# Sums of w2, score steps and one softmax put at other places in the planned order of a one-core attention and expert-layer kernel

## The chip, the cores and the metric

The kernel runs on one core of a Trainium2 chip. The metric is the device time of one execution in microseconds; of several runs the median counts. The core has a matrix engine (PE), three elementwise engines (DVE, ACT, POOL) and queues from which transfers are issued (SP above all, POOL and ACT too). Each engine and each queue works through its instructions strictly in the order in which they were written.

## The reference

All numbers are float32. Eight batches of 576 rows go through an attention with 32 memory slots per head, and the result (4608 rows of 512) through four experts with 1024 hidden values each:

```python
a = softmax(phi, axis=2)                          # over the sequence
k_m = einsum('bhsm,bhsd->bhmd', a, k)
v_m = einsum('bhsm,bhsd->bhmd', a, v)
attn = softmax(q @ k_m.T / sqrt(64))
x = (attn @ v_m) as (4608, 512)
p = domain_probs / sum(domain_probs)
for e in range(4):
    out += p[:, e:e+1] * (relu(x @ w1[e]) @ w2[e])
```

## The kernel before

**Products.** Each float32 operand is split into a rounded part and a rest ("high" and "low"), and each product is made of three matmuls (high by high, high by low, low by high). ACT rounds (a cast), DVE or POOL subtracts to get the rest. The product v_m·w1 is made first (`vw`), so that `x @ w1` becomes one product of `vw` with the transposed attention (`AT`).

**Steps.** The work is a list of 512 steps: 4 pairs of batches, 4 experts, 2 batches, 2 halves of a batch (256 and 320 rows), 8 blocks of the hidden layer. `PAIR` is 128 steps. In step s PE makes the hidden block of step s+2 (`first`, L669 to L671; ACT makes the high part with a relu at L681, DVE the low part at L683) and the second product of step s (`second`, L702 to L704). From step 192 on (`BEGIN`) another scheme runs (`unit`, L1041), which makes seven products in place of eight and needs sums and differences of the quarter blocks of w2.

**Work in between.** Everything else is put at step numbers in a table (`plan`), and `run_plan(s)` emits it at the start of step s. Steps 0 to 35 are ordered by a scheduler; from step 36 on the order is the written one. Three tables matter here.

- `JOBS`: (expert, half, step, home, lag). Each job is a call of `sums` (L189): at its step SP loads two blocks of w2 into a tile `raw` (L207, in one of three tiles with the tag `AT`); after `lag` steps DVE makes two sums and two differences in place (L231 to L234, POOL for the last job); in the four steps that follow ACT casts the high parts into a tile `sv` (L219) whose memory is named by `home`, POOL subtracts the rest (L220), and POOL's queue stores both (L225). The home `tl` borrows tiles of the attention.
- `ATT`: for batches 2 to 7 the steps of the attention: the load of phi, `turn` (transposes of the softmaxed phi, then the products with k and v from `turn` + 2 on: a split of the loaded kv by ACT, L351, and POOL, L352, and two steps later the product, L363), the writing of v_m, three score steps (L463; then a copy, a transpose, the maximum, the exponential, the sum and the scaling in the six steps behind it), and three transposes of the result (L541).
- `stage_ahead` (L134): kv, q and the weights to be split are loaded by SP into four stage tiles, in the order in which the plan takes them, three ahead of the one taken. A load waits until the tile used four loads before it is free again.

**Start.** The first batch's attention is written out by hand (from L1163 on). There `scores_exp`, `vw_out` of the first head pair and `soft` follow each other.

Of the kernel before, what the change touches and what calls it, by code (L numbers as in the profile page):

```python
# [10 lines left out]
F32R = mybir.dt.float32r  # L11
# [7 lines left out]
N, DM, E, F = 4608, 512, 4, 1024  # L19
P = 128  # L20
# [8 lines left out]
PAIR = E * STEPS  # L29
LAST = NG * PAIR  # L30
STAGE = 4
KVS = 3
# [18 lines left out]
PAIR_AT = ((18, 19, 26, 27), (28, 29, 30, 31))  # L51

ATT = {
    2: (22, 30, 48, (101, 107, 112), (114, 115, 119)),
    3: (38, 46, 65, (116, 118, 120), (PAIR + 2, PAIR + 4, PAIR + 6)),
    4: (88, 96, 114, (PAIR + 71, PAIR + 75, PAIR + 79), (PAIR + 81, PAIR + 85, PAIR + 93)),
    5: (107, PAIR - 2, PAIR + 16, (PAIR + 83, PAIR + 87, PAIR + 91), (PAIR + 118, PAIR + 124, PAIR + 128)),
    6: (PAIR + 3, PAIR + 14, PAIR + 32, (2 * PAIR + 99, 2 * PAIR + 103, 2 * PAIR + 107), (2 * PAIR + 109, 2 * PAIR + 113, 2 * PAIR + 117)),
    7: (PAIR + 18, PAIR + 32, PAIR + 50, (2 * PAIR + 111, 2 * PAIR + 115, 2 * PAIR + 119), (2 * PAIR + 125, 2 * PAIR + 127, 2 * PAIR + 128)),
}  # L60

UNITS_1 = (1, 5, 5, 6, 5, 6, 8, 9, 10, 11, 11, 12, 17, 13, 13, 20)
# [8 lines left out]
Q = 256  # L71
X_BANK, Y_BANK, AB_BANK = 4, 2, 6
JOBS = (
    (2, 0, 34, "w1", 5), (2, 1, 60, "tl", 4), (3, 0, 85, "w1", 5), (3, 1, 104, "kvs", 5),
    (0, 0, PAIR + 2, "w1", 5), (0, 1, PAIR + 33, "w1", 5), (1, 0, PAIR + 48, "kvs", 4),
    (1, 1, PAIR + 62, "kvs", 4),
)
KEEP_AT, W2_AGAIN = (20, 12, -1, 20), 24
FOUR_AT_7 = ((0, 4, 8, 12), (16, 20, 24, 28))
# [6 lines left out]
def body(ctx: ExitStack, tc: tile.TileContext, qm, qt, kv, kvt, phi, prob, w1, w1d, w2, out):  # L86
    nc = tc.nc
    pool = lambda name, **k: ctx.enter_context(tc.tile_pool(name=name, bufs=1, **k))
    const, wp, work, att = pool("const"), pool("wp"), pool("work"), pool("att")
# [103 lines left out]
    def sums(e, fh, s, home, lag):  # L193

        kept = []
        top, low = slice(0, Q), slice(Q, DM)
        late = s + lag > BEGIN
        v = nc.gpsimd if late else nc.vector
        sub = v.tensor_sub

        def load():
            tag = {"tag": "a"} if home == "tl" else {"tag": "AT", "bufs": 3}
            t = att.tile([P, 2, 2, DM], F32R, name="raw", **tag)
            kept.extend(t[:, i].bitcast(F32) for i in range(2))
            kept.append(t)
            for i in range(2):
                nc.sync.dma_start(kept[i], w2[e, 2 * fh + i])  # L207

        def high(i, j):
            if j == 0:  # L210
                if home == "tl":
                    width, tag = ((DM, "tl"), (640, "ph"))[i]
                    t = att.tile([P, 2, width], F32R, name="sv", tag=tag)
                    t = t.rearrange("p a c -> p (a c)")[:, :2 * DM].rearrange("p (a c) -> p a c", a=2)
                else:
                    pool, bufs = (wp, 4) if home == "w1" else (att, KVS)
                    t = pool.tile([P, 2, DM], F32R, name="sv", tag=home, bufs=bufs)
                kept.append(t)
            nc.scalar.copy(kept[3 + i][:, j], kept[i][:, j])  # L219
            nc.gpsimd.tensor_sub(kept[2][:, i, j], kept[i][:, j], kept[3 + i][:, j].bitcast(F32))  # L220

        def store(i):
            d = dram.tile([P, 2, 2, DM], F32, name=f"v{e}{fh}{i}")
            for r, src in enumerate((kept[3 + i], kept[2][:, i])):
                nc.gpsimd.dma_start(d[:, :, r], src.bitcast(F32))  # L225
            for j in range(2):
                kept_for["v", e, fh, 2 * i + j] = d[:, j]

        at(s, load)
        s += lag  # L230
        at(s, lambda: v.tensor_add(kept[1][:, :, low], kept[0][:, :, low], kept[1][:, :, low]))  # L231
        at(s + late, lambda: sub(kept[0][:, :, low], kept[0][:, :, top], kept[0][:, :, low]))
        at(s + 1 + late, lambda: sub(kept[0][:, :, top], kept[1][:, :, low], kept[0][:, :, top]))
        at(s + 1 + 2 * late, lambda: sub(kept[1][:, :, top], kept[1][:, :, top], kept[0][:, :, top]))  # L234
        s += 3 * late
        for i in range(2):
            for j in range(2):
                at(s + 1 + 2 * i + j, lambda i=i, j=j: high(i, j))
            at(s + 3 + 2 * i, lambda i=i: store(i))
# [211 lines left out]
    def tiles(t0):  # L451
        return (2, P) if t0 < 4 else (1, 64)
# [45 lines left out]
    def scores_exp(b, t0):  # L498
        nt, n = tiles(t0)
        av = st["at", b, t0][:n, :nt * H, :]  # L500
        nc.scalar.activation(av, av, AF.Exp, scale=float(D) ** -0.5)

    def soft_sum(b, t0):
        nt, n = tiles(t0)
        av = st["at", b, t0][:n, :nt * H, :]
        zv = st["mx", b, t0][:n, :nt * H]
        nc.vector.reduce_sum(guarded[:n, :nt * H, 0], av, AX.X)
        nc.vector.reduce_sum(zv[:, :, 0], guarded[:n, :nt * H], AX.X)
        nc.vector.reciprocal(zv[:, :, 0], zv[:, :, 0])
# [6 lines left out]
    def soft(b, t0):  # L516
        soft_sum(b, t0)
        soft_scale(b, t0, nc.vector)
# [59 lines left out]
    def vw_out(ps, k, e, fh, hp, odds, last=True):  # L578
        to = [(vw_tile(k, e, odd, fh, hp // 2), vw_rows(2 * k + odd, hp)) for odd in odds]
        for t, r in to:  # L580
            nc.scalar.copy(t[r, 0, :], ps[r])
        for t, r in to:
            nc.vector.tensor_sub(t[r, 1, :], ps[r], t[r, 0, :].bitcast(F32))  # L583
        if last:
            give(ps)
# [146 lines left out]
    def at(s, unit):  # L732
        plan[s].append(unit if isinstance(unit, tuple) else (None, unit))
# [427 lines left out]
    with tc.manual_schedule():  # L1161
        raw = {key: take(later) for later, key in enumerate(early)}
        stage_ahead(len(early) + 4)  # L1163
        nc.scalar.copy(att.tile([P, 1], F32, name="woken", tag="woken"), ident[:, :1])
        nc.sync.dma_start(pt, prob)
        keep_warm(10)
        dve, gps = nc.vector, nc.gpsimd
        for g in range(2):
            phi_max(0, g)
        for g in range(2):  # L1170
            phi_exp(0, g)
        kvr = lambda hp: raw["kv", 0, hp]
        for g in range(2):
            phi_norm(0, g)
        kv_split(0, 0, kvr(0), 0, gps)
        kv_split(0, 0, kvr(0), 1, dve)
        phi_turn(0, 0)
        phi_turn_out(0, 0)
        tail_split(0, raw["kvt", 0], 0, gps)
        phi_turn(0, 1)  # L1180
        phi_turn_out(0, 1)
        kv_split(0, 1, kvr(1), 0, dve)
        kv_split(0, 1, kvr(1), 1, gps)
        phi_turn_tail(0)
        phi_turn_tail_out(0)
        tail_split(0, raw["kvt", 0], 1, gps)
        for c2 in range(2):
            kv_split(0, 2, kvr(2), c2, dve)
        kv_split(0, 3, kvr(3), 0, dve)
        for hp in range(2):  # L1190
            for c2 in range(2):
                kv_mm(0, hp, c2)
            kv_mm_tail(0, hp)
        kv_split(0, 3, kvr(3), 1, dve)
        for hp in range(2):
            kv_out(0, hp)
        for hp in (2, 3):
            for c2 in range(2):
                kv_mm(0, hp, c2)
            kv_mm_tail(0, hp)  # L1200
            if hp == 2:
                for i in range(2):
                    kv_fold(0, i)
        keep_warm(3)
        kv_pick(0, 0)
        w1g = [raw["w1", 0, 0, g] for g in range(2)]
        split_w1(w1g[0], 0, 0, gps)
        for hp in (2, 3):
            kv_out(0, hp)
        write_vt_0(0, slice(0, 1))  # L1210
        q = raw["qm", 0, 0]
        scores_mm(0, 0, q, (0, 1))
        for hp in (2, 3):
            kv_fold(0, hp)
        keep_warm(5)
        kv_pick(0, 1)
        scores_mm(0, 0, q, (2, 3))
        scores_copy(0, 0)
        scores_turn(0, 0)
        scores_max(0, 0)  # L1220
        split_w1(w1g[0], 0, 1, gps)
        write_vt_0(0, slice(1, 2))
        keep_warm(2)
        split_w1(w1g[1], 0, 2, gps)
        split_w1(w1g[1], 0, 3, gps)
        pv = [vw_mm(0, 0, hp, ("p2", 4)) for hp in range(4)]
        scores_exp(0, 0)
        vw_out(pv[0], 0, 0, 0, 0, (0,))
        soft(0, 0)
        keep_warm(3)  # L1230
        for hp in (1, 2):
            vw_out(pv[hp], 0, 0, 0, hp, (0,))
        transposes(0, 0)
        keep_warm(4)
        transposes_out(0, 0)
        vw_out(pv[3], 0, 0, 0, 3, (0,))
        for i in range(2):
            split_w2(0, 0, i, raw["w2", 0, 0], gps)
        for s in range(AHEAD):
            first(s)  # L1240
        probabilities()
# [78 lines left out]
```

## Time and profile before

| What | Value |
|---|---|
| Median of 3 runs | 1383.67 us (1383.65 to 1386.94) |
| The profiled execution's own time | 1382.22 us |
| Its span, first to last instruction | 1380.4 us |
| PE's mean granted clock | 0.993 |
| Instructions | 26287 |
| Read from and written to memory | 221.85 MB, 84.93 MB |

The page gives each engine's busy time. The windows view gives the same by stretches, with the granted clock (PEclk) as a share of full speed. The timeline lists instructions in order of time: start, duration, engine, line, operation, tiles, and in square brackets how long the engine was idle before it and what ended that. Step 60 falls at about 230 us, step 98 at 329 us and step 110 at 367 us.

### The profile page before, as it was taken

How to read it: one execution, taken by the hardware profiler on the slowest of the kernel's cores; microseconds unless marked ns; L12 is line 12 of the kernel's file. 1: busy time of each engine (PE TensorE's matmuls, PEld its weight loads, DVE VectorE, ACT ScalarE, POOL GpSimd, SP SyncE). 2: the span in 40 equal slices, each digit the busy share in tenths (PEclk: the TensorE clock that was granted, in tenths of full speed). 3: DMA queues.
4: the chain of work that ended last, by engine and by line, in shares of the span. 5: the costliest groups of instructions: out<-in, count | busy, mean ns of one | idle time of the engine just before them, and what ended most of it. 6: DMA issues, size and time to landing. Idle time of an engine off the chain costs nothing.

```text
span 1380.4 us, 26287 instructions
## 1 busy us (share of the span) xinstructions
PE 1348.2 (98%) x9294; PEld 1237.0 (90%) x9294; DVE 852.1 (62%) x1920; ACT 658.0 (48%) x1594; POOL 693.8 (50%) x743
## 2 busy tenths in 40 slices
PE   7999999899899999999999999999999999999998
PEld 6778888787778888889999999999999999999998
DVE  7875635343545445457767766666667766666666
ACT  7765565445445655444445455555543333333332
POOL 4400474757443634446467677767754434334432
PEclk9999999999999999999999999999999999999999
DMA  6752375897578354464589999999983866666552
GB/s 258 250 187 76 116 247 180 310 311 240 164 255 295 123 179 155 168 248 150 176 275 317 373 331 320 320 311 325 340 282 130 255 178 180 180 182 177 168 172 75
DMA packets 104340, 309.84 MB, mean 224 GB/s; under 512 B 25232, under 2 KB 26384, under 8 KB 104208
## 3 DMA queue, kind: packets, MB, share of 16 engines
q1 hardware_dynamic: 83472, 232.65, 53.6%
q0 software_dynamic: 19584, 71.31, 13.2%
q10 hardware_dynamic: 1152, 4.19, 0.8%
q8 instruction: 74, 1.21, 0.4%
q14 instruction: 58, 0.48, 0.1%
HBM read 221.85 MB, written 84.93 MB: 222 GB/s over the span
## 4 chain that ended last, share of the span: by engine, by line
PE 86%; DVE 5%; issue 3%; POOL 2%; ACT 2%; DMA 1%; POOLq 0%; ACTq 0%; DVEq 0%
PE banks L1041 28%; PE banks L702 6%; PE banks L704 6%; PE banks L703 6%; PE banks L955 6%; PE banks L956 6%; PE banks L957 6%; PE banks L669 3%; PE banks L670 3%; PE banks L671 3%; PE banks L607 2%; PE banks L363 2%; DVE vw L583 1%; PE banks L1080 1%; PE banks L1079 1%
## 5 line engine op out<-in xcount | busy, mean ns | idle before, releaser
L1059 DVE SCALAR_TENSOR_TENSOR acc<-banks,pt,acc 128x256 f32<-128x256 f32 x528 | 253.0, 479 | 137.0 <-PE banks L1041 132.5
L164 POOL TENSOR_TENSOR w<-stage,w 128x512 fp32r<-128x512 f32 x134 | 175.4, 1315 | 141.2 <-ACT w L163 133.0
L1041 PE MATMUL banks<-w,a 128*128 128x256 f32 x1344 | 192.4, 282 | 0.0
L955 PE MATMUL banks<-AT,vw 128*128 128x256 f32 (+1 forms) x640 | 189.3, 296 | 0.0
L956 PE MATMUL banks<-AT,vw 128*128 128x256 f32 (+1 forms) x640 | 188.9, 295 | 0.0
L957 PE MATMUL banks<-AT,vw 128*128 128x256 f32 (+1 forms) x640 | 188.9, 295 | 0.0
L1041 PEld LDWEIGHTS banks<-w,a 128*128 128x128 f32 x1344 | 178.8, 189 | 4.9
L683 DVE SCALAR_TENSOR_TENSOR h<-banks,h 128x256 fp32r<-128x256 f32 x192 | 80.6, 420 | 132.3 <-ACT h L681 84.7
L1022 POOL TENSOR_TENSOR vt<-ph,vt 128x512 fp32r<-128x512 f32 x80 | 103.4, 1292 | 114.9 <-ACT vt L1021 84.6
L702 PE MATMUL banks<-w,h 128*128 128x512 f32 x384 | 152.8, 398 | 1.7 <-ACT h L681 1.7
L703 PE MATMUL banks<-w,h 128*128 128x512 f32 x384 | 152.1, 396 | 0.7 <-POOL w L164 0.7
L704 PE MATMUL banks<-w,h 128*128 128x512 f32 x384 | 151.5, 395 | 0.8 <-DVE h L683 0.8
L681 ACT ACTIVATE h<-banks 128x256 fp32r<-128x256 f32 x192 | 73.4, 383 | 124.1 <-PE banks L671 104.5
L1007 ACT ACTIVATE a<-banks 128x512 fp32r<-128x512 f32 x80 | 47.9, 598 | 173.4 <-DVE ph L1013 130.5
L1032 POOL TENSOR_TENSOR tl<-xs,tl 128x256 fp32r<-128x256 f32 x80 | 59.1, 739 | 133.3 <-ACT tl L1031 72.4
L669 PE MATMUL banks<-AT,vw 128*128 128x320 f32 (+1 forms) x384 | 118.8, 310 | 5.3 <-DVE h L683 3.0
L956 PEld LDWEIGHTS banks<-AT,vw 128*128 128x128 f32 x640 | 120.7, 189 | 0.1
L955 PEld LDWEIGHTS banks<-AT,vw 128*128 128x128 f32 x640 | 120.5, 188 | 0.2
L957 PEld LDWEIGHTS banks<-AT,vw 128*128 128x128 f32 x640 | 120.3, 188 | 0.0
L352 POOL TENSOR_TENSOR kvs<-stage,kvs 128x512 fp32r<-128x512 f32 x58 | 75.3, 1317 | 87.1 <-ACT kvs L351 80.0
L670 PE MATMUL banks<-AT,vw 128*128 128x320 f32 (+1 forms) x384 | 114.4, 298 | 0.0
L671 PE MATMUL banks<-AT,vw 128*128 128x320 f32 (+1 forms) x384 | 113.9, 298 | 0.0
(154 smaller groups left out, 3128.0 us busy)
## 6 DMA issues: line engine op xcount, KB each, us to landing
w<-kw SPq DMA_DIRECT2D x92, 512.0 KB, 5.2
vwd<-vst POOLq DMA_DIRECT2D x80, 512.0 KB, 6.4
vw<-vwd SPq DMA_DIRECT2D x320, 128.0 KB, 5.8
w<-v SPq DMA_DIRECT2D x68, 512.0 KB, 5.9
stage<-in_w SPq DMA_DIRECT2D x44, 512.0 KB, 4.5
stage<-in_w1d SPq DMA_DIRECT2D x40, 512.0 KB, 5.2
stage<-in_kv SPq DMA_DIRECT2D x32, 512.0 KB, 4.4
kw<-w POOLq DMA_DIRECT2D x24, 512.0 KB, 5.1
```

The costliest lines, as they stand in the source:

```text
L164: eng.tensor_sub(dst[:, 1, :], raw, dst[:, 0, :].bitcast(F32))
L669: nc.tensor.matmul(ps, w[:, 0, f], at_t[:, g, 0, c], start=g == 0, stop=False)
L670: nc.tensor.matmul(ps, w[:, 0, f], at_t[:, g, 1, c], start=False, stop=False)
L671: nc.tensor.matmul(ps, w[:, 1, f], at_t[:, g, 0, c], start=False, stop=g == 1)
L702: nc.tensor.matmul(po[t], x[:, 0, :], w[:, 0, :], start=j == 0, stop=False)
L703: nc.tensor.matmul(po[t], x[:, 0, :], w[:, 1, :], start=False, stop=False)
L704: nc.tensor.matmul(po[t], x[:, 1, :], w[:, 0, :], start=False, stop=j == NJ - 1)
L955: nc.tensor.matmul(ps, w[:, 0, f], at_t[:, g, 0, c], start=g == 0, stop=False)
L956: nc.tensor.matmul(ps, w[:, 0, f], at_t[:, g, 1, c], start=False, stop=False)
L957: nc.tensor.matmul(ps, w[:, 1, f], at_t[:, g, 0, c], start=False, stop=g == 1)
L1041: nc.tensor.matmul(ps, a[:, l, jj], w[:, r, c], start=start and jj + i == 0, stop=jj == 1 and i == 2, skip_group_check=True,)
L1059: VE.scalar_tensor_tensor(a, src, p, a, ALU.mult, ALU.add)
```

## The change

No matmul, cast or subtraction is added or removed; the softmax sums are the same. What changes is where the work stands.

```diff
-    2: (22, 30, 48, (101, 107, 112), (114, 115, 119)),
+    2: (22, 30, 48, (93, 97, 102), (111, 112, 113)),
...
-    (2, 0, 34, "w1", 5), (2, 1, 60, "tl", 4), (3, 0, 85, "w1", 5), (3, 1, 104, "kvs", 5),
+    (2, 0, 18, "kvs", 3), (2, 1, 34, "w1", 5), (3, 0, 85, "w1", 5), (3, 1, 98, "w1", 5),
...
-            tag = {"tag": "a"} if home == "tl" else {"tag": "AT", "bufs": 3}
-            t = att.tile([P, 2, 2, DM], F32R, name="raw", **tag)
+            t = att.tile([P, 2, 2, DM], F32R, name="raw", tag="AT", bufs=3)
...
         scores_exp(0, 0)
+        soft(0, 0)
         vw_out(pv[0], 0, 0, 0, 0, (0,))
-        soft(0, 0)
```

- **Jobs.** Expert 2's first job goes from step 34 to 18 (home kvs, lag 3), its second from step 60 (home tl) to the freed step 34; expert 3's second from 104 to 98 (home w1). The branch for the home tl is deleted. Three later jobs stand three steps earlier: steps 158, 173 and 187, the last with a lag of 6 instead of 4.
- **Batch 2.** Scores at steps 93, 97, 102 instead of 101, 107, 112; transposes at 111, 112, 113 instead of 114, 115, 119.
- **Batch 4.** `turn` goes from step 96 to 99, with all that hangs on it.
- **Batches 4 to 7, after step 192.** Score steps mostly five apart instead of four, with the transposes shifted by one to eight steps.
- **Start.** The softmax of the first scores stands ahead of the first `vw_out`.

On POOL, at steps 94 to 104. The tiles `w` are weights being split, `kvs` and `tl` the kv of batch 4, `at` the scores of batch 2, `raw` the sums of w2. Before:

```order
L164 TENSOR_TENSOR w_3407<-stage,w_3407 128x512
L164 TENSOR_TENSOR w_3432<-stage,w_3432 128x512
L338 TENSOR_TENSOR tl<-stage,tl 64x512 x2
L164 TENSOR_TENSOR w_3463<-stage,w_3463 128x512
L352 TENSOR_TENSOR kvs<-stage,kvs 128x512 x2
L164 TENSOR_TENSOR w_3495<-stage,w_3495 128x512
L164 TENSOR_TENSOR w_3515<-stage,w_3515 128x512
L352 TENSOR_TENSOR kvs<-stage,kvs 128x512 x4
```

and now:

```order
L164 TENSOR_TENSOR w_3425<-stage,w_3425 128x512
L164 TENSOR_TENSOR w_3449<-stage,w_3449 128x512
L164 TENSOR_TENSOR w_3482<-stage,w_3482 128x512
L164 TENSOR_TENSOR w_3508<-stage,w_3508 128x512
L508 TENSOR_TENSOR at<-at,mx 128x512
L164 TENSOR_TENSOR w_3536<-stage,w_3536 128x512
L332 TENSOR_TENSOR tl<-stage,tl 64x512 x2
L346 TENSOR_TENSOR kvs<-stage,kvs 128x512 x2
L508 TENSOR_TENSOR at<-at,mx 128x512
L346 TENSOR_TENSOR kvs<-stage,kvs 128x512 x2
L214 TENSOR_TENSOR raw<-raw,sv 128x512 x2
```

The first kv splits now stand behind all weight splits of this stretch, and the subtractions of expert 3's second job stand among the kv splits.

On SP, at steps 92 to 100. `vw` are tiles read back from memory, `in_qm` is q, `in_kvt` and `in_kv` the kv of batch 4, `raw` the blocks of w2. Before:

```order
L646 DMA vw<-vwd_3242 32x1024
L149 DMA stage<-in_kv 128x1024
L149 DMA stage<-in_w 128x1024
L149 DMA stage<-in_qm 128x1024
L149 DMA stage<-in_kv 128x1024 x2
```

and now:

```order
L640 DMA vw<-vwd_3242 32x1024
L149 DMA stage<-in_qm 128x1024
L149 DMA stage<-in_w 128x1024
L149 DMA stage<-in_kvt 128x1024
L149 DMA stage<-in_kv 128x1024
L206 DMA raw<-in_w 128x1024 x2
L149 DMA stage<-in_qt 128x256
```

The load that stood first behind the `vw` loads was kv; in its place, and so in its stage tile, now stands the q of batch 2's second score step.

On ACT, at steps 110 and 111. `h` and `hm` are the relus that the second product waits for, `sv` the casts of a w2 job, `at` the exponential of the scores, `ph,zs` that of phi. Before:

```order
L163 CAST w_3826<-stage 128x512
L376 COPY xs<-banks 64x128 x2
L219 CAST sv<-raw 128x512
L681 ACTIVATE hm<-banks 128x64
L681 ACTIVATE h<-banks 128x256
L163 CAST w_3864<-stage 128x512
L501 ACTIVATE at<-at 128x512
L281 ACTIVATE ph,zs<-ph,nm 128x576 x2
L219 CAST sv<-raw 128x512
```

and now:

```order
L163 CAST w_3856<-stage 128x512
L370 COPY xs<-banks 64x128 x2
L345 CAST kvs<-stage 128x512 x2
L385 COPY kvm_78<-banks 128x128
L675 ACTIVATE hm<-banks 128x64
L675 ACTIVATE h<-banks 128x256
L163 CAST w_3895<-stage 128x512
L275 ACTIVATE ph,zs<-ph,nm 128x576 x2
```

The two casts `sv` and the exponential `at` are gone from here; a kv split and a copy have come.

More of the change, by code (lines that the diff above doesn't have):

```diff
@@ L53 @@
 ATT = {
-    2: (22, 30, 48, (101, 107, 112), (114, 115, 119)),
+    2: (22, 30, 48, (93, 97, 102), (111, 112, 113)),
     3: (38, 46, 65, (116, 118, 120), (PAIR + 2, PAIR + 4, PAIR + 6)),
[L56 to L59, printed above, removed]
+    4: (88, 99, 117, (PAIR + 71, PAIR + 76, PAIR + 81), (PAIR + 79, PAIR + 84, PAIR + 94)),
+    5: (107, PAIR - 2, PAIR + 16, (PAIR + 86, PAIR + 91, PAIR + 96), (PAIR + 118, PAIR + 124, PAIR + 128)),
+    6: (PAIR + 3, PAIR + 14, PAIR + 32, (2 * PAIR + 99, 2 * PAIR + 103, 2 * PAIR + 108), (2 * PAIR + 110, 2 * PAIR + 114, 2 * PAIR + 118)),
+    7: (PAIR + 18, PAIR + 32, PAIR + 50, (2 * PAIR + 112, 2 * PAIR + 116, 2 * PAIR + 123), (2 * PAIR + 120, 2 * PAIR + 125, 2 * PAIR + 131)),
 }
@@ L73 @@
 JOBS = (
-    (2, 0, 34, "w1", 5), (2, 1, 60, "tl", 4), (3, 0, 85, "w1", 5), (3, 1, 104, "kvs", 5),
-    (0, 0, PAIR + 2, "w1", 5), (0, 1, PAIR + 33, "w1", 5), (1, 0, PAIR + 48, "kvs", 4),
-    (1, 1, PAIR + 62, "kvs", 4),
+    (2, 0, 18, "kvs", 3), (2, 1, 34, "w1", 5), (3, 0, 85, "w1", 5), (3, 1, 98, "w1", 5),
+    (0, 0, PAIR + 2, "w1", 5), (0, 1, PAIR + 30, "w1", 5), (1, 0, PAIR + 45, "kvs", 4),
+    (1, 1, PAIR + 59, "kvs", 6),
 )
@@ L210, in high @@
             if j == 0:
[L211 to L217, printed above, removed]
+                pool, bufs = (wp, 4) if home == "w1" else (att, KVS)
+                t = pool.tile([P, 2, DM], F32R, name="sv", tag=home, bufs=bufs)
                 kept.append(t)
```

## The prediction, made before the changed kernel had run

> **What bounds the kernel now.** I read the page's busy times first, then its chain, then the windows, then the timeline of each engine wherever the windows show PE idle.
>
> ```profile
> PE 1348.2 (98%) x9294; PEld 1237.0 (90%) x9294; DVE 852.1 (62%) x1920; ACT 658.0 (48%) x1594; POOL 693.8 (50%) x743
> ...
> PE 86%; DVE 5%; issue 3%; POOL 2%; ACT 2%; DMA 1%; POOLq 0%; ACTq 0%; DVEq 0%
> ...
> 0.00:60.00 60.00, 49.42 (x307) 40.18 (x308) 47.06 (x95) 44.11 (x103) 25.09 (x28) 0.94 0.70 251
> 240.00:260.00 20.00, 15.98 (x87) 13.46 (x86) 7.83 (x17) 8.74 (x22) 18.83 (x21) 1.00 0.85 302
> 320.00:340.00 20.00, 16.59 (x96) 14.23 (x94) 6.18 (x15) 11.87 (x29) 19.65 (x18) 0.95 0.67 227
> 340.00:360.00 20.00, 20.00 (x138) 16.60 (x137) 7.21 (x20) 8.78 (x26) 7.10 (x6) 0.96 0.78 247
> 360.00:380.00 20.00, 16.49 (x98) 14.13 (x97) 10.91 (x28) 8.80 (x25) 9.26 (x9) 0.89 0.32 93
> 380.00:400.00 20.00, 18.86 (x105) 15.16 (x104) 8.77 (x24) 11.24 (x32) 10.04 (x11) 0.94 0.61 215
> 620.00:700.00 80.00, 78.50 (x672) 73.61 (x671) 58.63 (x140) 34.23 (x82) 44.28 (x49) 1.00 0.53 172
> 1060.00:1080.00 20.00, 18.99 (x163) 16.98 (x163) 15.15 (x37) 7.24 (x20) 8.85 (x10) 1.00 0.57 173
> ```
>
> A window's row gives its length, then the busy time of PE, weight loads, DVE, ACT and POOL, then PE's granted clock. PE is busy for 1348.2 of 1380.4 us and the change alters none of its work, so all it can win is the 32.2 us of idle PE and the stretches at a lowered clock. Those lie in few places: 10.6 us at the start, 4.0 at 240 to 260, 3.4 at 320 to 340, 3.5 and 1.1 at 360 to 400, 1.5 and 1.0 later. The clock is down at the start and from 320 to 400 only.
>
> **A: the w2 sum at step 60.** It moves away.
>
> ```profile
> 252.63 0.50 PE L703 MATMUL banks<-w,h 128*128 128x512 f32 x1 [0.67 <-POOL w L164]
> 257.65 0.50 PE L607 MATMUL banks<-w,vs 128*128 128x512 f32 x1 [3.36 <-POOL w L164]
> ...
> 249.88 0.62 ACT L163 CAST w<-stage 128x512 fp32r<-128x512 f32 x1
> ...
> 248.59 0.72 POOL L225 DMA_DIRECT2D v<-sv  x1
> 249.76 1.59 POOL L220 TENSOR_TENSOR raw<-raw,sv 128x512 fp32r<-128x512 f32 x1
> 254.64 0.93 POOL L225 DMA_DIRECT2D v<-sv  x1
> 255.82 1.78 POOL L164 TENSOR_TENSOR w<-stage,w 128x512 fp32r<-128x512 f32 x1
> ```
>
> PE waits twice, 0.67 and 3.36 us, for weight splits that POOL makes late. Ahead of them POOL does four subtractions of the job (1.3 to 1.6 us each) and four store issues (about 0.6 us each, the distance of the rows at 254.64 and 255.82 being two of them): 8 us in all. Without them the split of 255.82 is ready 8 us sooner, and what is late next is ACT's cast, done at 250.5, before PE asks at 253.9. **A is worth 4.0 us.**
>
> The job goes to step 34, where one of the same shape stood; that one goes to step 18.
>
> ```profile
> 136.10 1.28 POOL L338 TENSOR_TENSOR tl<-stage,tl 64x512 fp32r<-64x512 f32 x1 [57.68 <-ACT tl L337]
> ...
> 100.00:120.00 20.00, 20.00 (x106) 17.11 (x105) 8.13 (x22) 4.49 (x15) 0.00 (x0) 1.00 0.17 61
> ...
> 104.96 0.33 SPq L149 DMA_DIRECT2D stage<-in_w  x1
> 122.97 0.33 SPq L149 DMA_DIRECT2D stage<-in_w  x1
> ```
>
> POOL has nothing to do for 57.7 us there, and DVE and ACT are idle for 11.9 and 15.5 of the 20 us from 100 on, so four operations on each are hidden. If none were, DVE's four at 0.69 us would cost 2.8; I take 0. On SP the load for step 34 now stands between the two weight loads shown. It must wait until the first job's stores have freed its tile; from 104.96 to 122.97 SP has 18 us for that.
>
> **B: batch 4's kv product.**
>
> ```profile
> 336.13 0.74 PE L363 MATMUL banks<-kvs,a 128*128 128x256 f32 x4 [2.89 <-POOL kvs L352]
> 339.14 0.63 PE L702 MATMUL banks<-w,h 128*128 128x512 f32 x1
> ...
> 330.98 2.52 POOL L338 TENSOR_TENSOR tl<-stage,tl 64x512 fp32r<-64x512 f32 x2
> 333.59 1.26 POOL L164 TENSOR_TENSOR w<-stage,w 128x512 fp32r<-128x512 f32 x1
> 334.81 2.52 POOL L352 TENSOR_TENSOR kvs<-stage,kvs 128x512 fp32r<-128x512 f32 x2
> ...
> 333.75 0.62 ACT L163 CAST w<-stage 128x512 fp32r<-128x512 f32 x1 [3.70 <-DMA stage<-in_w]
> ```
>
> PE stands for 3.4 us (by the window) because POOL is behind, and then runs at half clock (a 512 matmul takes 0.63 us, 0.40 elsewhere). The windows from 320 to 360 lose 0.05 and 0.04 of 20 us, 1.8 us. **B costs 5.2 us.** The product now comes three steps of about 2.2 us later, with two score steps (about 0.9 us of PE each) ahead of it and 0.8 us of phi transposes already there before: near 341 us on the old scale instead of 333. POOL, from 330.9 on, has four weight splits (5.2), one scaling (1.05), two tl (2.5) and two kvs (2.5) to do: done at 342 at the latest, and the product's first half needs only the first of the two kvs. I count B as gone, with nothing to spare; bounds 0 to 5.2.
>
> **The q of step 97 is new there.** SP's load behind the `vw` loads waits for the stage tile of a weight block that POOL splits at steps 93 and 94.
>
> ```profile
> 324.51 0.35 SPq L149 DMA_DIRECT2D stage<-in_kv  x1
> 326.01 0.60 PE L307 MATMUL banks<-ident,ph 128*128 128x128 f32 x4
> ...
> stage<-in_qm SPq DMA_DIRECT2D x16, 512.0 KB, 4.7
> ```
>
> Before, this was kv and had time. Now it is q, issued at 324.5 and landed 4.7 us later (median of the q loads) at 329.2. PE, whose step 97 began with the row at 326.01, asks at 326.6 (a score step and its transpose, 0.9, less one phi transpose, 0.35, come ahead). **I expect a new wait of 2.5 us**, 0 if POOL gets there sooner, 4.6 with the slowest load of that stretch (6.8 us). It gives POOL the time that B lacked.
>
> Whether the clock falls with it is open: 3.36 us of idle left it at 1.00 in 240 to 260, 2.89 lowered it at 336. The Trainium skill, page "TensorE: Matmul & The Clock Gate", section "Part 1: The HAM clock gate", says that the clock halves after an idle window of about 3.4 us, and that the windows run free of the program. The trace agrees that length alone does not decide. By that rule a wait of 2.5 us leaves the clock alone and the sum below stands; by the row at 336 it would be 1.8 us more.
>
> **C: steps 110 to 112.**
>
> ```profile
> 376.55 0.64 PE L669 MATMUL banks<-AT,vw 128*128 128x320 f32 x1 [3.01 <-DVE h L683]
> ...
> 370.55 0.68 DVE L233 TENSOR_TENSOR raw<-raw 128x512 f32<-128x512 f32 x1
> ...
> 371.31 0.62 ACT L219 CAST sv<-raw 128x512 fp32r<-128x512 f32 x1 [3.36 <-issue]
> 373.38 0.77 ACT L281 ACTIVATE ph<-ph,nm 128x576 f32<-128x576 f32 x1
> 375.52 0.38 ACT L681 ACTIVATE h<-banks 128x256 fp32r<-128x256 f32 x1
> ```
>
> ACT stands 3.4 us before a cast of expert 3's second job, whose input DVE makes only at 371.2, behind scores and phi maxima. The relus wait behind that cast, and then behind two exponentials of phi, one of scores and another cast; PE idles 3.5 us in this window. The clock loses 0.11 and 0.06 of 20 us, 3.4, of which up to 1.5 falls into idle time: 1.9 to 3.4, I take 2.6. **C costs 6.1 us.** The job's casts go to steps 104 to 107 and the scores earlier, so phi's exponentials stand alone. What comes in at 110 (a kv split of 1.2 us and a copy) fits a step. At 104 the same wait exists in small: ACT's first cast stands behind DVE's accumulation. I take C as gone and 1.0 us as the price of the fuller steps 101 to 113 (bounds 0 and 5.2, a stall like B).
>
> **Small terms.** At 380 to 400 PE idles 1.1 us beside batch 2's transposes and scores, which leave: 1.0 won. At the start:
>
> ```profile
> 29.67 0.66 PE L541 MATMUL banks<-ident,at 128*128 128x128 f32 x4 [2.49 <-DVE at L514]
> ...
> 26.23 0.68 DVE L583 TENSOR_TENSOR vw<-banks,vw 64x512 fp32r<-64x512 f32 x1
> 27.63 0.68 DVE L164 TENSOR_TENSOR w<-stage,w 128x512 fp32r<-128x512 f32 x1
> 28.39 0.63 DVE L164 TENSOR_TENSOR w<-stage,w 128x512 fp32r<-128x512 f32 x1
> ```
>
> Three pieces of other work, some 1.9 us, leave the softmax's way, but the eviction put behind it then stands ahead of the next thing PE needs: 0.8 won, bounds 0 and 2.5. The later score steps stand beside 1.5 and 1.0 us of idle; four of their waits cannot all go: 0.6 won, bounds -1 and 2.5.
>
> **Sum.** 4.0 + 5.2 + 6.1 + 1.0 + 0.8 + 0.6 = 17.7 won, 2.5 + 1.0 = 3.5 lost, 14.2 net. The profiled execution took 1382.2 us (span 1380.4 and 1.8 around it), so 1368.0; the median of the runs is 1.5 above it: **1369.5 us**.
>
> **Rivals.**
> - *One stall comes back*, as kv splits, sums and weights crowd POOL at 101 to 108, or with the q wait at half clock: 5.2 us, 1374.7. For it speaks that B's sum leaves nothing to spare.
> - *Everything goes well*: q in time, the start and the late steps at their upper bounds, 2.5 + 1.7 + 1.9 more: 1363.4. Against it speaks the row at 324.51.
> - *The amount, not the order, makes B and C*: POOL is busy for 19.65 of 20 us at 320 to 340, and what it must do by step 113 is the same. Then the stalls only move, and A and the small terms less the q wait remain, 3 us: 1380.5, within what can be told from no change. Against it: POOL is busy for only 7.1 of the next 20.
> - *Slower*: SP stands at the load for step 34 until the stores of step 18's job land, with two weight loads and all of batch 2's kv behind it. From 123 us on each us late may reach PE; it eats the gain at 137 and makes the kernel slower by over 0.3% (4.2 us, about what can be told from no change) at 141.5. With a landing 20 us late: 1375 to 1390. Against it: some 18 us of room.
>
> **How the numbers follow.** Forecast (1365 to 1372.5) 0.56; one stall back (1372.5 to 1379) 0.21; all well (1360 to 1365) 0.09; only moved (1379.5 to 1387.8) 0.09; slower 0.05. The first three are faster by over 0.3%: 0.86. The range leaves out a tenth at each end: 1362 to 1379.
>
> **What would show it.** The windows 240 to 260 and 350 to 390 with PE at 20.0 and the clock at 1.00 show A, B and C gone. A wait of step 97's score product on the load of q, of 1 to 4 us near 320 us, shows the new one. A wait of the kv product or of the hidden block on POOL or DVE near 335 to 350 us shows the first rival; SP idle past 123 us at the load of `raw` the last. The forecast is wrong if PE idles over 3 us at a place not named here.

## The result, and the profile after

| What | Before | After |
|---|---|---|
| Median of 4 runs | 1384.0 us (1383.65 to 1386.94) | 1369.43 us (1368.16 to 1369.53) |
| Ratio, 95% interval | | 0.9888 [0.9871, 0.9905] |
| Span of the profiled execution | 1380.4 us | 1367.6 us |

The forecast was 1369.5 us. That it is met this closely is luck: the start cost 7.5 us more than forecast, smaller terms came out better by 6.3 us together, and the place of the two profiled executions among the runs made up the rest (the sum is below). One execution of this study, the profiled one of the kernel e11_turn96, took 2179.74 us at a granted clock of 0.556; its ratio leaves that execution out, and no drift of it is given.

The page's busy times and windows of the changed kernel (length, busy PE, weight loads, DVE, ACT, POOL, then PE's granted clock, DMA share and GB/s):

```profile
PE 1346.5 (98%) x9294; PEld 1236.9 (90%) x9294; DVE 852.1 (62%) x1920; ACT 658.1 (48%) x1594; POOL 695.1 (51%) x743
...
60.00:80.00 20.00, 16.49 (x90) 13.86 (x89) 9.66 (x28) 10.23 (x31) 5.03 (x4) 0.83 0.69 244
240.00:260.00 20.00, 20.00 (x113) 17.56 (x112) 8.49 (x19) 10.09 (x25) 15.23 (x18) 1.00 0.80 282
320.00:340.00 20.00, 19.88 (x133) 16.88 (x134) 10.04 (x24) 14.64 (x34) 19.55 (x18) 1.00 0.89 299
340.00:360.00 20.00, 19.99 (x129) 17.55 (x128) 12.12 (x30) 10.50 (x33) 15.15 (x14) 1.00 0.87 285
360.00:380.00 20.00, 19.85 (x114) 17.34 (x114) 8.90 (x28) 12.42 (x36) 10.59 (x10) 1.00 0.47 166
380.00:400.00 20.00, 19.44 (x145) 15.54 (x144) 8.74 (x18) 7.26 (x21) 6.59 (x10) 1.00 0.60 213
```

From 240 to 400 the stalls are gone and the clock stays at 1.00. The window 60 to 80 lost 3.5 us of PE and has its clock at 0.83; before, it stood at 20.00 and 1.00. That stall was in no term of the forecast.

**The drift.** Where the time went is read more sharply from one instruction that both kernels run 192 times in the same order: DVE's low part of the relu of hidden block k. For block 18 the timelines of DVE say, before and after:

```profile
96.24 0.41 DVE L683 SCALAR_TENSOR_TENSOR h<-banks,h 128x256 fp32r<-128x256 f32 x1
```

```profile
102.89 0.41 DVE L677 SCALAR_TENSOR_TENSOR h<-banks,h 128x256 fp32r<-128x256 f32 x1
```

so the changed kernel is 6.65 us late there. The same difference at five more blocks (the expectations below call block k "step k"), in us against the kernel before:

```
block            9     18     72     81     90    123
changed       -0.1    6.7    6.9    2.0    2.0  -10.9
```

Between blocks 9 and 18 it loses 6.8, between 72 and 81 it wins 4.9 (A), between 90 and 123 it wins 12.9 (B, C and the small term), and behind block 123 another 1.9, to 12.8 in all, the difference of the spans. Between blocks 90 and 123 moved work cancels only at the end, so the figures within that stretch are not read one by one.

**The lost stretch.** Timelines of SP, ACT and PE in the changed kernel, from 59 to 70 us:

```profile
59.51 0.33 SPq L149 DMA_DIRECT2D stage<-in_w  x1
...
61.45 0.22 ACT L675 ACTIVATE hm<-banks 128x64 fp32r<-128x64 f32 x1
66.05 1.14 ACT L163 CAST w<-stage 128x512 fp32r<-128x512 f32 x2 [4.38 <-DMA stage<-in_w]
67.09 0.61 ACT L345 CAST kvs<-stage 128x512 fp32r<-128x512 f32 x1
67.61 0.53 ACT L370 COPY xs<-banks 64x128 f32<-64x128 f32 x2
...
68.19 0.48 PE L378 MATMUL banks<-ident,xs 128*128 128x128 f32 x1 [3.26 <-ACT xs L370]
69.58 0.63 PE L698 MATMUL banks<-w,h 128*128 128x512 f32 x1
```

PE waits 3.26 us for copies on ACT. ACT could have made them at 63.6, when PE had finished their banks, but it stands at two casts of a weight whose load was issued at 59.51, 6.5 us before they could begin. Then PE runs at about half its speed (a 512 matmul takes 0.63 us, 0.40 elsewhere; the clock of this window is 0.83). These are steps that the scheduler orders, and in the kernel before it had put the copies ahead of the second of these casts, and the load ahead of one of two phi loads.

### The profile page after: what moved, and what is told of

Same layout as the page of the kernel before. It is cut to its first block, busy times and chain, and to the rows that moved or that the text cites. A ratio compares the mean times of both kernels' runs of the same rounds, so it can differ in the third digit from the quotient of the medians.

```text
span 1367.6 us, 26263 instructions
## 1 busy us (share of the span) xinstructions
PE 1346.5 (98%) x9294; PEld 1236.9 (90%) x9294; DVE 852.1 (62%) x1920; ACT 658.1 (48%) x1594; POOL 695.1 (51%) x743
## 3 DMA queue, kind: packets, MB, share of 16 engines
q8 instruction: 74, 1.21, 0.4%
## 4 chain that ended last, share of the span: by engine, by line
PE 90%; DVE 4%; ACT 3%; DMA 2%; issue 2%; POOL 0%; SPq 0%; ACTq 0%; DVEq 0%; POOLq 0%
PE banks L1035 29%; PE banks L698 6%; PE banks L696 6%; PE banks L697 6%; PE banks L949 6%; PE banks L950 6%; PE banks L951 6%; PE banks L663 3%; PE banks L665 3%; PE banks L664 3%; PE banks L601 3%; PE banks L357 2%; PE banks L1074 1%; PE banks L1073 1%; PE banks L1075 1%
## 5 line engine op out<-in xcount | busy, mean ns | idle before, releaser
L663 PE MATMUL banks<-AT,vw 128*128 128x320 f32 (+1 forms) x384 | 118.3, 309 | 3.6 <-DVE vw L577 1.7
L1035 PE MATMUL banks<-w,vt 128*128 128x256 f32 x768 | 113.9, 281 | 0.2 <-DVE acc L1053 0.2
L664 PE MATMUL banks<-AT,vw 128*128 128x320 f32 (+1 forms) x384 | 113.3, 296 | 0.0
```

The costliest lines, as they stand in the source:

```text
L663: nc.tensor.matmul(ps, w[:, 0, f], at_t[:, g, 0, c], start=g == 0, stop=False)
L664: nc.tensor.matmul(ps, w[:, 0, f], at_t[:, g, 1, c], start=False, stop=False)
L1035: nc.tensor.matmul(ps, a[:, l, jj], w[:, r, c], start=start and jj + i == 0, stop=jj == 1 and i == 2, skip_group_check=True,)
```

## The experiments

The kernels of the experiments were each timed in five rounds against the kernel before. "Gain" is one minus the ratio, times 1384 us, with its 95% interval; A is the drift from block 72 to 81, "middle" that from 90 to 123, "start" that from 9 to 18 (negative is a gain), in one profiled execution each.

| Kernel | Median us | Gain us | start | A | middle |
|---|---|---|---|---|---|
| changed kernel | 1369.43 | 15.5 (13.1 to 17.9) | 6.8 | -4.9 | -12.9 |
| e1_noswap | 1364.36 | 18.0 (15.2 to 20.8) | 0.0 | -4.9 | -12.9 |
| e2_swap | 1389.5 | -5.3 (-7.1 to -3.5) | 7.1 | 1.2 | 0.2 |
| e3_sum | 1367.07 | 16.5 (14.7 to 18.3) | 1.6 | -4.9 | -13.0 |
| e12_problate | 1365.99 | 16.7 (13.4 to 20.1) | 0.5 | -4.9 | -13.0 |
| e4_jobs2 | 1377.99 | 5.8 (4.2 to 7.3) | 0.0 | -4.9 | 0.6 |
| e5_mid | 1372.78 | 11.5 (8.7 to 14.3) | 0.0 | 2.4 | -13.0 |
| e6_b2j3 | 1372.58 | 11.8 (9.6 to 14.1) | 0.0 | -0.3 | -11.5 |
| e7_phi4b2 | 1374.83 | 9.1 (7.1 to 11.1) | 0.0 | 1.3 | -9.1 |
| e9_b2 | 1374.31 | 10.4 (7.9 to 12.7) | 0.0 | 1.2 | -9.4 |
| e10_j3 | 1380.24 | 4.0 (2.6 to 5.5) | 0.0 | 2.3 | -4.8 |
| e8_late | 1382.76 | 1.4 (0.1 to 2.8) | 0.0 | 1.2 | -0.8 |
| e11_turn96 | 1366.57 | 18.7 (15.5 to 21.9) | | | |

Kernels that leave a stretch as it was show how far one execution scatters: A lies between -0.3 and 2.4 in them, "middle" between -0.8 and 0.6.

### The stall at 68 us

**e1_noswap**, the changed kernel without the swap:

```diff
-        soft(0, 0)
         vw_out(pv[0], 0, 0, 0, 0, (0,))
+        soft(0, 0)
```

> The changed kernel without the swap at the start (the eviction ahead of the softmax's sum again); all tables as in the change. Theory: the 3.26 us stall at 68 us and the half clock behind it, 6.7 us between the relus of steps 9 and 18, come from the swap, because the ordered steps 0 to 35 then come out in another order (two phi loads ahead of a weight load on SP, both casts of that weight ahead of four copies on ACT). Then this kernel loses the stall and keeps everything else: 1369.4 - 6.7 = 1362.7 us, 0 to 0.8 more for the start, and the window 60 to 80 has PE at 20.0 at clock 1.00. Rival: the stall comes from expert 2's first job, now at step 18, whose loads and stores crowd the same stretch: then it stays and the time is 1369 to 1371.

The stall is gone and the start drifts by 0.0; the median is 1364.36, against 1362.7 to 1363.5 expected.

**e2_swap**, the kernel before with the swap alone:

```diff
+        soft(0, 0)
         vw_out(pv[0], 0, 0, 0, 0, (0,))
-        soft(0, 0)
```

> The kernel before with the swap at the start alone. Theory (the swap makes the stall): 1384.0 + 6.7 = 1390.7 us, and PE waits 3 us for the copies of the kv product near 68 us. Rival (the job at step 18 makes it): within 1 us of before, 1383 to 1384, by the 0.8 us that the prediction gave the swap.

Slower by 5.3 us (3.5 to 7.1), with the same wait, in its timeline of PE:

```profile
70.31 0.47 PE L384 MATMUL banks<-ident,xs 128*128 128x128 f32 x1 [3.58 <-ACT xs L376]
```

The theory holds, the time a little below its 1390.7: the swap alone makes the stall, and no job is needed for it.

**e3_sum** keeps half of the swap and **e12_problate** all of it, and both come out of the scheduler in other orders:

```diff
-        soft(0, 0)
+        soft_sum(0, 0)
         vw_out(pv[0], 0, 0, 0, 0, (0,))
+        soft_scale(0, 0, nc.vector)
```

> The changed kernel with only the sum and the reciprocal of the softmax ahead of the eviction and its scaling behind it. On ACT the second pair of kv copies then stands ahead of the casts of the late weight again; on SP the two phi loads still stand ahead of that weight's load. Theory that ACT's order makes the stall: it is gone, 1362 to 1363.5. Rival that the later load alone makes it: the stall stays, smaller, and the time is 1366 to 1369.

```diff
-        probabilities()
     load_phi(1)
+    probabilities()
```

> The whole changed kernel, the swap included, with one line moved: the normalisation of the expert probabilities (DVE) stands behind the load of batch 1's phi instead of ahead of it. The computation is the same; the ordered steps come out in a third order, in which the four copies and the relus stand ahead of the casts of the late weight on ACT, while the two phi loads still stand ahead of that weight's load on SP. Theory (ACT's order makes the 3.3 us stall, and the swap itself wins some 1.6 us at the start): the stall near 68 us is gone, 1363 to 1365. Rival (the later load costs by itself, as the 1.6 us left between steps 9 and 18 with the scaling put behind): 1366 to 1367.5.

In both the long stall is gone. e12_problate separates the two suspects best, in its timelines of SP and ACT:

```profile
61.92 0.33 SPq L149 DMA_DIRECT2D stage<-in_w  x1
...
65.56 0.53 ACT L376 COPY xs<-banks 64x128 f32<-64x128 f32 x2 [0.93 <-PE banks L366]
...
68.13 1.17 ACT L163 CAST w<-stage 128x512 fp32r<-128x512 f32 x2
```

The load is issued at 61.92, behind the two phi loads as in the changed kernel and no earlier than there (2.4 us later, of which 2.0 are this execution's lateness at block 9). But the copies stand ahead of the casts on ACT, and between blocks 9 and 18 only 0.5 us is lost. So with the load as late as that, ACT's order decides whether PE stalls. The casts in front of the copies with an early load were not tried. Measured from block 9, the changed kernel issues the load 1.7 us later than the kernel before (59.51 for 57.90); by an estimate from these rows the earlier load would have taken about half of the 3.26 us away.

Both medians (1367.07, 1365.99) miss the times of the theory (1362 to 1363.5, 1363 to 1365) and lie at those of the rivals (1366 to 1369, 1366 to 1367.5), though the stall by which the theory and the rival were told apart is gone. They stay above that of the kernel without the swap; the intervals of the three gains overlap. In the profiles nothing is left for e12_problate, whose span is 1363.0 us against 1363.2 without the swap; e3_sum still loses 1.6 us between blocks 9 and 18. Whether the rest of the medians is more than scatter was not tried.

### A: expert 2's jobs

```diff
-    (2, 0, 34, "w1", 5), (2, 1, 60, "tl", 4), ...
+    (2, 0, 18, "kvs", 3), (2, 1, 34, "w1", 5), ...
```

> The kernel before with expert 2's two jobs alone moved (34 to 18, 60 to 34; the branch for the home tl stays in the text, unused). Theory: A alone, 4.0 us by the prediction, 4.6 to 4.9 by the drift of the relus between steps 72 and 81 of the changed kernel: 1379.1 to 1380. Rival (step 18 crowds SP or the clock): 1384 or more.

Faster by 5.8 us (4.2 to 7.3), drift 4.9; the theory holds, somewhat above its size. The other stalls are untouched: the kv product still waits 2.91 us and the hidden block at 374.58 still 3.01.

### B and C: the moves around step 100

**e5_mid** makes all three moves, without the swap and expert 2's jobs:

```diff
-    2: (22, 30, 48, (101, 107, 112), (114, 115, 119)),
+    2: (22, 30, 48, (93, 97, 102), (111, 112, 113)),
-    4: (88, 96, 114, ...),
+    4: (88, 99, 117, ...),
-    (3, 1, 104, "kvs", 5),
+    (3, 1, 98, "w1", 5),
```

> The kernel before with the three moves around step 100 together: batch 2's score steps and transposes, batch 4's turn three steps later, expert 3's second job at 98. Theory (B, C and the small term won, no wait for q): the relus drift by 12.9 us between steps 90 and 123 of the changed kernel, so 1384.0 - 12.9 = 1371 us. Rival (only moved, POOL's amount decides; the gain there needs the jobs of expert 2 out of the way): 1376 or more.

**e6_b2j3** leaves out the move of batch 4's turn (the two lines for 4):

> The kernel before with batch 2's score steps and transposes and expert 3's second job moved, batch 4's turn left at 96. Theory: C goes (6.1) and the small term (1.0), B stays (5.2 of the 12.3) and may grow, since the score steps now stand on POOL and ACT beside the kv product: 1384.0 - 7.1 = 1377 us, with a wait of the kv product on POOL near 334 us. Rival: once the scores are elsewhere the kv product is in time without being moved: 1371 to 1373.

**e7_phi4b2** leaves out the job's move (the last two lines):

> The kernel before with batch 2's score steps and transposes and batch 4's turn moved, expert 3's second job left at step 104. Theory: B goes (5.2) and the small term (1.0); of C the casts of the job stay where they block ACT, so its 3 us stall stays in part: 1384.0 - 6.2 to - 9, 1375 to 1378. Rival (the scores and exponentials of batch 2 alone made C): 1371 to 1372.

**e9_b2** makes the first move alone:

> The kernel before with batch 2's score steps and transposes moved alone; turn at 96 and expert 3's second job at 104 as before. Theory: the score work now ahead of the kv product is what covers POOL's lateness (the product waited 0.5 us with the turn at 96 and the job moved), so B goes, and of C half stays (3.5 us of idle stayed with the job at 104 in the run with the turn moved): 1384.0 - 7 to - 9 = 1375 to 1377 us, no wait over 1 us of the kv product near 338. Rival (the turn's move is needed while the job stands at 104): the kv product waits 2 to 3 us again and the time is 1379 or more.

**e10_j3** moves the job alone:

> The kernel before with expert 3's second job alone moved (104 to 98, home w1). Theory: the casts leave ACT's way at steps 110 to 112, but batch 2's exponential stays there: C goes in part, 3 to 4 of 6.1, B stays: 1380 to 1381. Rival 1: the job's subtractions and stores at step 103 on crowd POOL and the kv product waits longer: 1384 or more. Rival 2: the cast alone was the whole of C: 1378.

All three moves win 13.0 in the drift, as expected, and 11.5 us (8.7 to 14.3) in the times. For e6_b2j3 the theory fell and its rival holds: without the turn's move the middle still wins 11.5, and e9_b2 wins 9.4 with the scores alone. Why, its timelines of POOL and PE show:

```profile
338.05 2.56 POOL L352 TENSOR_TENSOR kvs<-stage,kvs 128x512 fp32r<-128x512 f32 x2 [0.21 <-ACT kvs L351]
...
339.60 0.74 PE L363 MATMUL banks<-kvs,a 128*128 128x256 f32 x5
340.67 0.62 PE L363 MATMUL banks<-kvs,a 128*128 128x256 f32 x3 [0.32 <-POOL kvs L352]
```

This kernel is 3.0 us late at block 90, so POOL begins the split at 335.05 on the scale of before, where it began it at 334.81: POOL is no earlier. PE comes later. It comes to the product at 336.6 on that scale; before, the wait of 2.89 us that ended at 336.13 had begun at 333.24. The score products, their transposes and a short wait of 0.67 us now lie ahead and fill the time that was idle. The times of e7_phi4b2 and e9_b2 (1374.83, 1374.31) came out just below those of their theories (1375 to 1378, 1375 to 1377), that of e10_j3 (1380.24) within.

C has two parts. With the scores moved and the job left at 104 (e9_b2), waits of 1.21 and 1.35 us stay at 374 to 380; with the job alone moved (e10_j3) one of 1.56 us stays at 381, and B with it, as its timeline of PE shows:

```profile
339.98 2.25 PE L363 MATMUL banks<-kvs,a 128*128 128x256 f32 x7 [3.17 <-POOL kvs L352]
```

What is left at 381 comes for the most part through DVE and not from the exponential of the scores. The timeline of ACT in e10_j3:

```profile
373.02 0.65 ACT L501 ACTIVATE at<-at 128x512 f32<-128x512 f32 x1
...
378.89 0.78 ACT L292 ACTIVATE ph<-ph,zs 128x576 f32<-128x576 f32 x1 [2.82 <-DVE zs L287]
```

The exponential still stands ahead of phi's, and with the casts gone the hidden block at 376.21 does not wait. The next relus stand behind the scaling of phi at 378.89, which waits 2.82 us for DVE. On DVE the sum of batch 2's softmax stands there from 377.38 on and takes 1.1 us; the exponential, 0.65 us long, can have delayed this chain by no more than some 0.5 (an estimate from these rows).

The two moves alone win 9.4 and 4.8, together 11.5. The turn's move adds 1.5 where the job stands at 98 (13.0 against 11.5) and takes 0.3, which is within the scatter, where it stands at 104 (9.1 against 9.4). No run has the turn's move alone. In the whole kernel:

```diff
-    4: (88, 99, 117, ...),
+    4: (88, 96, 114, ...),
```

> The changed kernel without the swap at the start and with batch 4's turn left at step 96 (written at 114). Theory: the turn's move is worth the 1.3 us by which the drifts of the runs with and without it differ (12.9 against 11.6 between steps 90 and 123): 1364.4 + 1.3 = 1365.7. Rival: with expert 2's job gone POOL is earlier and the move is worth nothing, 1364 to 1364.7, or it alone keeps the kv product from waiting, 1367 to 1370.

Its gain of 18.7 us (15.5 to 21.9) cannot be told from the 18.0 (15.2 to 20.8) with the turn at 99: this run decides nothing about 1 to 2 us.

### The late moves

```diff
-    (0, 1, PAIR + 33, "w1", 5), (1, 0, PAIR + 48, "kvs", 4),
-    (1, 1, PAIR + 62, "kvs", 4),
+    (0, 1, PAIR + 30, "w1", 5), (1, 0, PAIR + 45, "kvs", 4),
+    (1, 1, PAIR + 59, "kvs", 6),
```

and the late score steps and transposes of batches 4 to 7, alone:

> The kernel before with the late moves alone (the three jobs of step 158 and later, the score steps and transposes of batches 4 to 7 after step 192). Theory: what the changed kernel gains behind step 123, 1.9 us by the drift (0.6 by the prediction): 1382.1. Rival: no change, 1383.5 to 1384.5, the 1.9 being due to another place of the transfers.

1.4 us (0.1 to 2.8): a small gain, compatible with 0.6 and with 1.9. The profiles tell more. Behind block 123 this execution wins 1.9 us on that of the kernel before, and the changed kernel and the three made from it (e1_noswap, e3_sum, e12_problate) win 1.7 to 1.9. But the seven kernels without them (e2_swap, e4_jobs2 to e7_phi4b2, e9_b2, e10_j3) win 0.7 to 1.3 there too, 1.1 on average; about that much, it seems, the profiled execution of the kernel before was slow in that stretch. By an estimate from these means the late moves are worth about 0.7 us.

## Why the prediction was right, point by point

The time was met, and A, B and C went as forecast. But by a sign that the prediction itself gave, "the forecast is wrong if PE idles over 3 us at a place not named here", the forecast was wrong in one place: PE idles 3.26 us at 68 us, where it expected nothing.

- **A, 4.0 us.** Right in mechanism, a little low: 4.9 in the drift, 5.8 in the times. The step that was mis-sized counted only the idle time shown. In the timeline 512 matmuls that last 0.40 us follow each other every 0.23, so each wait hides some 0.17 us more than its bracket; 0.3 for the two waits; the other 0.6 of the drift was not traced. And behind the stall the clock was at 1.00 in the execution read, which is not so in all.
- **The job at step 18, and the slower rival.** Hidden, as argued: e4_jobs2 drifts by 0.0 at the start, and in the changed kernel nothing is late behind SP's load for step 34: PE idles 0.95 us in two waits at 143 to 147 us where it idled 0.70 at 136 to 140.
- **B, 5.2 us.** Gone, but its working gave the cause half to the turn's three steps. They are not needed: the two score steps ahead of the product do it (e9_b2, e6_b2j3). Whether the three steps alone would do it was not tried.
- **The wait for q, 2.5 us.** It did not come. The step that failed is "SP's load behind the `vw` loads waits for the stage tile of a weight block that POOL splits at steps 93 and 94". The changed kernel's timelines of PE and SP:

```profile
319.28 0.66 PE L457 MATMUL banks<-stage,kvm 64*32 64x256 f32 x16
328.85 0.66 PE L457 MATMUL banks<-stage,kvm 64*32 64x256 f32 x16
...
320.04 0.35 SPq L149 DMA_DIRECT2D stage<-in_qm  x1
```

  The load of q is issued at 320.04, 0.1 us after the score product of step 93 ends (319.28 + 0.66), and the trace puts SP's wait before it down to PE (0.6 us, line L457), not to POOL. There are four stage tiles in turn, and the q of step 93 is itself a new entry in that turn: it shifts every later load by one tile. The prediction read the tile's release off the order of before. PE asks at 328.85, 8.8 us after the issue; it waits for nothing.
- **C, 6.1 us, the small term, 1.0, and the crowding, -1.0.** B, C and the small term were put at 12.3 together and measured 12.9 (13.0 in e5_mid). So no price of the fuller steps is seen: PE idles 0.15 us at 360 to 380. The reason given for C was casts and exponentials in ACT's order. For the job's casts the runs bear it out: without them (e10_j3) the wait of 3.01 us is gone, and where they stay (e9_b2) relus still come late. The exponential of the scores alone delays no hidden block directly behind it; most of what batch 2's scores add is the wait through DVE shown above, which the prediction did not name.
- **The start, 0.8 won.** This is the term that failed most: "three pieces of other work ... leave the softmax's way, but the eviction put behind it then stands ahead of the next thing PE needs". That chain was read rightly as far as it goes, the wait for the first transposes fell from 2.49 to 1.27 us:

```profile
28.68 0.98 PE L535 MATMUL banks<-ident,at 128*128 128x128 f32 x4 [1.27 <-DVE at L508]
```

  But the working stopped at the lines moved. Steps 0 to 35 are ordered by a scheduler, the swap gave another order 35 us later, and that cost 6.8 us in the drift and 5.3 (3.5 to 7.1) in the times.
- **The late moves, 0.6.** Within what e8_late shows, and near the 0.7 of the profiles.
- **The sum.** Against the forecast's 14.2, 7.5 us more were lost at the start (6.7 by block 18 in place of 0.8 won) and 0.2 up to block 72. For it, 2.5 (q), 1.0 (crowding), 0.9 (A), 0.6 (B and C) and 1.3 (late, 1.9 for 0.6; most of it, it seems, from the slow stretch of the execution before), 6.3 in all. That leaves 12.8, the difference of the spans. The medians differ by 14.6, since the profiled execution of before (1382.22) lies 1.8 us below its median and that of after (1369.49) at its median. The forecast had put the latter at 1368.0 and its median 1.5 above it: the two errors cancel, by luck.
- **The rivals.** *The amount, not the order* is refuted by the window 320 to 340: POOL is busy for 19.55 of 20 us, as before (19.65), and PE no longer waits. *Everything goes well* gave 1363.4, near what the kernel without the swap reaches (1364.36), but by other terms: it counted a start won at its upper bound. *One stall comes back* happened at a place that it did not name, at its price (5.2 forecast, 5.3 measured by e2_swap) but not at its time, 1374.7, since the wait for q and the crowding stayed away.

The best kernel of this study is the change without the swap at the start: 1364.36 us, ratio 0.987 [0.985, 0.989] to before. That it beats the whole change rests on e2_swap's interval and on the missing stall; the two were not timed side by side.

## What to carry to other kernels

Where any part of a program is ordered by a scheduler, a line moved in a hand-written part can change the order elsewhere; compare the built order of every engine over the whole scheduled part, not only around the edit, and look for an in-order engine that now stands at a load ahead of something short that PE needs. A transfer that goes into tiles used in turn has to be followed through the new order: one entry more shifts every later load to another tile, with another releaser. And a stall behind a late engine can be filled as well as shortened: putting PE's own work ahead of the product removed B without making POOL earlier.

## What the runs showed of the hardware

The same stall has different prices. A's wait stands in the kernel before and in seven of the experiments with the same 3.36 or 3.37 us, ended by the same split on POOL. Behind it, the windows of e6_b2j3, e9_b2 and e5_mid show the clock at 1.00, 0.91 and 0.85:

```profile
260.00:280.00 20.00, 20.00 (x104) 17.42 (x103) 9.04 (x24) 10.34 (x29) 12.20 (x14) 1.00 0.91 303
```

```profile
260.00:280.00 20.00, 20.00 (x97) 17.38 (x96) 7.95 (x20) 9.58 (x26) 11.98 (x13) 0.91 0.91 303
```

```profile
260.00:280.00 20.00, 19.88 (x90) 17.38 (x91) 7.48 (x18) 9.29 (x24) 11.41 (x14) 0.85 0.93 306
```

Against the kernel before, A's stretch then takes 0.3 us less, 1.2 more and 2.4 more; so by an estimate what removing A is worth runs from 4.6 to 7.3 us in single executions (4.9 less 0.3 to 4.9 plus 2.4), which is how 4.9 in the drift and 5.8 in the times can go together. The like holds for B: in e4_jobs2 its 2.91 us of idle are followed by a clock of 0.83 in 320 to 340 and 1.00 in the next window, a loss of 3.4 us, where before the two windows had 0.95 and 0.96, a loss of 1.8:

```profile
320.00:340.00 20.00, 17.07 (x100) 14.06 (x98) 5.82 (x12) 10.90 (x26) 18.13 (x16) 0.83 0.75 242
```

The Trainium skill, page "TensorE: Matmul & The Clock Gate", section "Part 1: The HAM clock gate (the "warmup" mystery)", says that the clock falls to half after at least one idle window of about 3.4 us, and that these windows run free of the program. The spread over equal waits agrees with windows that run free, while the 2.91 us above shows that an idle time shorter than such a window was enough here.

The start is as uneven: the kernels that open with the same instructions in the same order as the kernel before reach block 9 between 0.4 and 2.5 us later than its profiled execution. A gain of 0.8 us there, as forecast for the swap, can't be read from one profile; the three with the whole swap reach it 0.1 us earlier (the changed kernel), 1.7 and 1.9 us later (e2_swap, e12_problate).
